# Small TensorE pieces in program order between blocks of matrix products: an attention, two-layer and expert kernel on one Trainium2 core

## The chip, the core and the metric

One NeuronCore of a Trainium2 chip runs the whole program; the other seven are idle. The metric is the device time of one execution in microseconds (us). TensorE multiplies, ScalarE (ACT in the profile), VectorE (DVE) and GpSimd (POOL) do the elementwise work, SyncE (SP) issues most DMAs.

## What is computed

All tensors are float32. Cut to what matters:

```python
def sm_attn(qq, kk, vv):
    s = scale * np.matmul(qq, kk.transpose(0, 1, 3, 2))
    a = softmax(s)
    return np.matmul(a, vv)
p_packed = sm_attn(p, k, v)              # 8 batches, 8 heads, 32 packed rows
x = sm_attn(q, p_packed, p_packed)       # 576 queries a batch -> 4608 tokens of 512
h = x @ w_in                             # 512 -> 2048
x = np.maximum(0.01 * h, h) @ w_out      # 2048 -> 512
logits = x @ w_gate                      # 8 experts
# greedy assignment, 576 tokens an expert, by falling logit
out[mask] = np.maximum(x[mask] @ w1[e], 0.0) @ w2[e]
```

## The kernel before

The program has four parts. `packs` makes the packed rows of all batches and folds them into `w_in` (tensor `wp` in DRAM). `tokens` (line 1383), which the change is about, does the query attention and the two layers for batches 0 to 5 and the first layer of batches 6 and 7. Then comes routing, in whose gaps TensorE does the second layer of batches 6 and 7 (`PutOff`), and last the eight experts.

Products are made exact enough by splitting each operand into a high and a low part and adding three products. In `tokens` the loops are batch `b` and, inside, 16 slices `f` of 128 of the 2048 hidden columns. For each slice:

- `mm1` (line 887): the first layer, 12 products of 288 columns (lines 54 to 56) into two PSUM banks of tile `h`; ScalarE copies them out, VectorE applies the slope, `split` (line 901) makes the halves `g`. This is a **block** of first-layer products.
- `mm2_list`: the second layer of the slice before, 12 products of 512 columns on even batches and 15 on odd ones (line 1044), into the accumulators `acc`, the fifth of which is the pool `a5` (tile `acc5`). Even batches do not use that fifth bank. They are queued in `todo`, and `emit` issues some.

Between the blocks lie **small pieces**, all of which pass through one PSUM bank, tile `x`:

- the query side of a later batch, `q_side` (line 783): per half, five pieces: two groups of four transposes of `rows` (line 547), two transposes of the tail (line 553), two score products (line 812, two each); then a softmax on ScalarE, VectorE and GpSimd (lines 820 to 836) into tile `at`, which that batch's `mm1` reads. GpSimd reorders the raw rows first (line 65).
- `times_gate` (line 1018): `turn` transposes 128 rows (line 1027), ScalarE copies them to `rowt` (line 1029), `product` multiplies by the gate weights (line 1034), VectorE copies the result to `L` or `wog` (line 1035). It is done for the finished rows of a batch (queue `dots`) and for 16 slices of `w_out` (queue `gates`, `wog_pieces`).
- `logits` (line 931): gate products for the batches whose second layer is put off; VectorE adds them to `lg` (line 956).

`evac` (line 993) copies the accumulators to `row` tiles at a batch's end. `side_unit` does `mm1` for batches 6 and 7 in the later slices of batches 4 and 5, and `SIDE_Q` says where their query sides are queued.

What sets the order: the program is recorded, and a list scheduler with a cost model orders each engine's instructions. In `tokens` it does so for TensorE too: `ordered(tc, MT)` with `MT` False leaves it free. Pieces are taken from the queues `qs`, `tabs`, `gates` and `dots` in the loop over `f`, one of each at a time.

Of the kernel before, what the change touches and what calls it, by code (L numbers as in the profile page):

```python
# [28 lines left out]
class Lag:  # L29
# [12 lines left out]

    def drain(self):
        self.pop(len(self.q))


def mm3(nc, ps, pairs, first=True, last=True):
# [431 lines left out]


LATE = 2
GPOP = 1
WI, WO, QS = 2, 5, 3
WOP = 2
W0 = 4
# [8 lines left out]
U6, U7 = 66, 84  # L494
LF = 16
DP = 0
SIDE_Q = [(2, 8), (4, 4)]


def SIDE(b, f):  # L500
# [253 lines left out]
class Tokens:  # L754
# [28 lines left out]
    def q_side(self, b, pool=None):  # L783

        nc, P = self.nc, self.P
        V, A, G, PE = nc.vector, nc.scalar, nc.gpsimd, nc.tensor
        st = {}

        def x_tile(shape):
            return P.ps.tile(shape, F32, name="x")  # L790

        def load(g):
            st[g] = load_rows(self.tc, nc, P.one, self.q, b, g, "")

        def rows(g):
            m, t = st[g]
            r = P.one.tile([128, 4, 4, 64], F32, name="rows")
            by_row(nc, r, m)
            qt = P.one.tile([128, 2, S], F32, name="kt", tag="kt")
            st["qt"] = qt  # L800
            st["fns"] = pairs_t(nc, qt, r, t, self.ident, x_tile, 64)
            st["fns"][0]()

        def sc(g, hf):
            qt = st["qt"]
            if hf == 0:
                t = P.two.tile([128, S], F32, name="soft", tag="soft")
                st["s"] = t
            ps = x_tile([128, HS])
            cs = slice(hf * HS, (hf + 1) * HS)  # L810
            for j in range(2):
                PE.matmul(ps[64 * j:64 * j + 64], self.cpp[:, b // 2, 2 * g + j, (b % 2) * 64:(b % 2) * 64 + 64],
                          qt[:, j, cs], start=True, stop=True)
            V.transpose(st["s"][:, cs], ps)

        def sm(g):
            nb = S // 32
            sf = st["s"]
            s = sf.rearrange("p (a b) -> p a b", b=32)
            mx = P.two.tile([128, nb], F32, name="mx2")  # L820
            V.reduce_max(mx, s, axis=AX.X)
            (G if PS & 1 else V).tensor_sub(s, s, mx.unsqueeze(2).to_broadcast([128, nb, 32]))
            A.activation(s, s, AF.Exp, scale=0.125)
            sm_ = P.two.tile([128, nb], F32, name="sm2")
            V.reduce_sum(sm_, s, axis=AX.X)
            V.tensor_scalar(sm_, sm_, 1e-9, None, op0=OP.add)
            V.reciprocal(sm_, sm_)
            (G if PS & 2 else V).tensor_mul(s, s, sm_.unsqueeze(2).to_broadcast([128, nb, 32]))
            e = P.two.tile([128, S], F32, name="soft", tag="soft")
            V.transpose(e, sf)  # L830
            if g == 0:
                t = (pool or P.two).tile([128, 2, 2, S], F32R, name="at2", tag="at2")
                st["at"] = t
            at = st["at"]
            A.copy(at[:, 0, g], e)
            V.tensor_sub(at[:, 1, g], e, f32(at[:, 0, g]))  # L836

        fns = [lambda: load(0)]
        for g in range(2):
            fns += [lambda g=g: rows(g), lambda: st["fns"][1](), lambda g=g: (st["fns"][2](), g == 0 and load(1)),  # L840
                    lambda g=g: sc(g, 0), lambda g=g: sc(g, 1), lambda g=g: sm(g)]
        return st, fns

    def open(self, keep, st):

        tc, nc = self.tc, self.nc

        def pool(st, name, bufs):
            return st.enter_context(tc.tile_pool(name=name, bufs=bufs, side="right"))

        self.wk5, self.wk3 = pool(keep, "t5", T1), pool(keep, "t3", 3)
        k1 = pool(keep, "k1", 1)
        self.lg, self.dots = {}, Lag()
# [77 lines left out]
    def logits(self, b, f, tf):  # L931
# [11 lines left out]
            nc.gpsimd.memset(t, 0.0)  # L943
            self.lg[b] = t
        lg = self.lg[b]
        ps = self.P.ps.tile([128, 192], F32, name="x")
# [67 lines left out]
    def gate(self, x, col):  # L1014

        self.dots.add(self.times_gate(lambda: x, lambda: self.L[:, col]))

    def times_gate(self, rows, out):

        nc, PE = self.nc, self.nc.tensor  # L1020
        st = {}

        def turn():
            x = rows()
            ps = self.P.ps.tile([128, 4, 128], F32, name="x")
            for c in range(4):
                PE.transpose(ps[:, c], x[:, c * 128:(c + 1) * 128], self.ident)
            st["t"] = self.two.tile([128, 4, 128], F32, name="rowt")
            nc.scalar.copy(st["t"], ps)

        def product():
            ps = self.P.ps.tile([128, E], F32, name="x")
# [3 lines left out]
        return [turn, product]  # L1036


def mm2_list(nc, acc, g, tl, wh, wl, start, stop):
# [343 lines left out]
def tokens(tk, pk, keep, first, st, acc_pools):  # L1383
# [5 lines left out]
    at = tk.first  # L1389
    tk.open(keep, st)  # L1390
    w = tk.w
    qs, tabs, gates = Lag(), Lag(), Lag()
    gates.add(tk.wog_pieces())
    tabs.add(tk.table_pieces)
    todo = []
    side = [(b, f) for b in range(B - ND, B) for f in range(NF)]
    sd = dict(at=[], w=None, next=0)

    def emit(n):
        for _ in range(min(n, len(todo))):  # L1400
            todo.pop(0)()

    def side_q():
        b = B - ND + len(sd["at"])
        at, fns = tk.q_side(b, tk.one)
        sd["at"].append(at)
        qs.add(fns)
        if b == B - ND:
            sd["w"] = tk.wp_load1(b, 0)

    def side_unit():
        b, f = side[sd["next"]]
# [9 lines left out]
    for b in range(B - ND):  # L1422
        if b == 1:
            first.close()
            tk.open_gate(keep, st)
        if b + 1 < B - ND:
            nat, fns = tk.q_side(b + 1)
            qs.add(fns)
        for f in range(NF):
            if b == 0 and f < NF - WOP:  # L1430
                for i in range(2):
                    tk.wout_piece(pk.w64, WOP + f, i)
            if f % 2 == 0:
                wcur = w
                nb, nf = (b, f // 2 + 1) if f // 2 < 7 else (b + 1, 0)
                if nb < B - ND:
                    if nb == 0:
                        pk.need(nf)
                    else:
                        pk.rest()  # L1440
                    w = tk.wp_load(nb, nf)
            t = tk.mm1(at, wcur, slice((f % 2) * 128, (f % 2) * 128 + 128))
            g, tl = tk.split(b, f, t)
            if b == 0:
                for _ in range(PI):
                    pk.piece()
                for _ in range(PP):
                    emit(PM)
                    pk.part()
            n = -(-len(qs.q) // (NF - f)) if b else QP  # L1450
            qs.pop(min(n, 1))
            if b:
                tabs.pop(1)
                gates.pop(GPOP)
            emit(len(todo) // 2)
            tk.dots.pop(1)
            if n > 1:
                emit(len(todo) // 2)
                qs.pop(n - 1)
            emit(len(todo))  # L1460
            if (b, f) == (B - ND - 1, LF):
                later.load(2)
            if f == 0:
                acc = sums(acc_pools, b)
            todo += mm2_list(nc, acc, g, tl, tk.wo(f, 0), tk.wo(f, 1), f == 0, f == NF - 1)
            if b == B - ND - 1:
                todo.append(lambda b=b, f=f, t=t: tk.logits(b, f, t))
            if f == NF - 1:
                todo.append(lambda b=b, acc=acc: tk.evac(b, acc, b < B - ND - 1))
            if (b, f) in SIDE_Q:  # L1470
                side_q()
            if SIDE(b, f):
                lg = side_unit()
                emit(len(todo) // 2)
                todo.append(lg)
        if b + 1 < B - ND:
            qs.drain()
            at = nat
    while sd["next"] < len(side):
        lg = side_unit()  # L1480
        emit(len(todo))
        tk.dots.pop(1)
        for _ in range(FTAIL):
            later.one()
        todo.append(lg)
    emit(len(todo))
    tk.dots.drain()
    return later


# [77 lines left out]
```

## Time and profile before

| | us |
|---|---|
| median of 3 runs (1464.46 to 1470.62) | 1464.66 |
| the profiled execution, its own time | 1474.13 |
| its span, first to last instruction | 1472.4 |
| TensorE busy in the span | 1381.9 |
| ScalarE, VectorE, GpSimd busy | 560.1, 742.3, 299.7 |
| mean granted TensorE clock, share of 2.4 GHz | 0.959 |

The page gives busy time by engine and the span in 40 slices. The windows view gives the same for chosen stretches; batches 1 to 5 of `tokens` lie between 258 and 864 us, routing between about 890 and 1020, the experts behind it. A busy TensorE is not TensorE at its peak: at the half clock the same product takes longer and still counts as busy.

### The profile page before, as it was taken

What the parts mean: (1) busy time and instruction counts of PE and PEld (TensorE: products, weight loads), DVE (VectorE), ACT (ScalarE), POOL (GpSimd) and SP (SyncE); (2) the same over time, 40 slices, a digit from 0 to 9 for tenths busy, and PEclk for the clock granted to TensorE, in tenths of its full rate; (3) what the DMA queues carried; (4) which work ended last, traced back from release to release, by engine and by line L of the source; (5) the groups of instructions that cost most, each with busy time, mean ns of one, the idle gap of its engine ahead of it and who ended that gap; (6) DMA issues with size and microseconds to landing.
All of it is one profiled execution on the core that took longest, in us unless ns stands there. A gap on an engine that the chain in (4) does not pass through costs nothing. (4 is left out here: it accounts for less than half of the span.)

```text
span 1472.4 us, 25686 instructions
## 1 busy us (share of the span) xinstructions
PE 1381.9 (94%) x10206; PEld 1150.2 (78%) x10206; DVE 742.3 (50%) x1878; ACT 560.1 (38%) x1209; POOL 299.7 (20%) x293
## 2 busy tenths in 40 slices
PE   7998898999998998899999988898999999999997
PEld 4666776887887886787788876676898989898986
DVE  4775798443343442356645566685444343433341
ACT  5665455433444443354544440101333332333331
POOL 3222224211212221232211120001221220220111
PEclk9999999998897997799999999998999999999999
DMA  9997655202102111133322354544643443443320
GB/s 272 292 276 222 196 170 179 81 29 66 35 30 71 43 37 49 45 122 121 129 76 93 109 196 160 158 141 124 198 124 106 129 136 108 136 116 100 122 72 36
DMA packets 147881, 180.49 MB, mean 123 GB/s; under 512 B 27952, under 2 KB 105776, under 8 KB 147760
## 3 DMA queue, kind: packets, MB, share of 16 engines
q1 hardware_dynamic: 122992, 141.08, 31.2%
q10 hardware_dynamic: 19008, 18.88, 4.3%
q0 software_dynamic: 5760, 18.88, 3.8%
q8 instruction: 81, 1.33, 0.4%
q14 instruction: 40, 0.33, 0.1%
HBM read 124.27 MB, written 54.53 MB: 121 GB/s over the span
## 5 line engine op out<-in xcount | busy, mean ns | idle before, releaser
L1044 PE MATMUL acc<-wout,g 128*128 128x512 f32 x1728 | 451.2, 406 | 14.8 <-ACT wout L778 5.5
L1044 PEld LDWEIGHTS acc<-wout,g 128*128 128x128 f32 x1728 | 316.5, 191 | 86.7 <-ACT wout L778 8.1
L898 DVE SCALAR_TENSOR_TENSOR t<-t 128x576 f32<-128x576 f32 x128 | 102.9, 804 | 142.8 <-ACT t L897 142.6
L897 ACT COPY t<-h 128x288 f32<-128x288 f32 x256 | 99.1, 400 | 169.2 <-PE h L56 147.7
L54 PE MATMUL h<-xt,w1hl 128*128 128x288 f32 x504 | 148.4, 294 | 1.4 <-DVE eg__12322 L1178 1.4
L55 PE MATMUL h<-xt,w1hl 128*128 128x288 f32 x504 | 148.5, 295 | 0.0
L56 PE MATMUL h<-xt,w1hl 128*128 128x288 f32 x504 | 148.4, 294 | 0.0
L54 PE MATMUL h<-at,wphl 128*128 128x288 f32 x384 | 122.2, 320 | 1.6 <-ACT t L897 1.4
L55 PE MATMUL h<-at,wphl 128*128 128x288 f32 x384 | 117.6, 306 | 0.2 <-DVE at L836 0.2
L56 PE MATMUL h<-at,wphl 128*128 128x288 f32 x384 | 116.3, 304 | 0.3 <-POOL wphl L875 0.3
L875 POOL TENSOR_TENSOR wphl<-wpraw,wphl 128x512 fp32r<-128x512 f32 x48 | 67.8, 1412 | 225.5 <-ACT wphl L874 225.3
L912 DVE TENSOR_TENSOR g<-t,g 128x512 fp32r<-128x512 f32 (+1 forms) x96 | 82.0, 854 | 42.7 <-ACT g L909 42.4
L54 PEld LDWEIGHTS h<-xt,w1hl 128*128 128x128 f32 x504 | 94.6, 188 | 4.3 <-ACT w1hl L1059 1.8
L55 PEld LDWEIGHTS h<-xt,w1hl 128*128 128x128 f32 x504 | 94.6, 188 | 2.4
L56 PEld LDWEIGHTS h<-xt,w1hl 128*128 128x128 f32 x504 | 94.5, 188 | 0.0
L1120 POOL DMA_INDIRECT xg<-x2d,idx x36 | 34.5, 960 | 289.7 <-PE x L1143 145.9
L54 PEld LDWEIGHTS h<-at,wphl 128*128 128x128 f32 x384 | 74.7, 196 | 9.5 <-ACT t L897 2.0
L909 ACT CAST g<-t 128x512 fp32r<-128x512 f32 (+1 forms) x96 | 64.7, 674 | 43.3 <-DVE t L898 42.4
L55 PEld LDWEIGHTS h<-at,wphl 128*128 128x128 f32 x384 | 75.2, 196 | 5.8 <-DVE at L836 0.9
L1183 POOL DMA_INDIRECT out_dram<-ot,idx x32 | 43.9, 1371 | 171.5 <-DVE ot L1196 163.9
L56 PEld LDWEIGHTS h<-at,wphl 128*128 128x128 f32 x384 | 74.9, 195 | 0.7 <-POOL wphl L875 0.5
L1070 DVE TENSOR_TENSOR w2hl<-w2raw,w2hl 128x1024 fp32r<-128x1024 f32 x31 | 37.9, 1224 | 59.6 <-ACT w2hl L1069 59.4
(778 smaller groups left out, 2444.9 us busy)
## 6 DMA issues: line engine op xcount, KB each, us to landing
gd<-g SPq DMA_DIRECT2D x32, 576.0 KB, 3.2
wp<-ev ACTq DMA_DIRECT2D x64, 256.0 KB, 4.8
w1raw<-in_moe_w_dram SPq DMA_DIRECT2D x30, 512.0 KB, 3.4
w2raw<-in_moe_w_dram SPq DMA_DIRECT2D x30, 512.0 KB, 3.6
wpraw<-wp SPq DMA_DIRECT2D x48, 256.0 KB, 2.9
g<-gd SPq DMA_DIRECT2D x16, 576.0 KB, 4.3
rawk<-in_k_dram SPq DMA_DIRECT2D x16, 512.0 KB, 5.8
rawv<-in_v_dram SPq DMA_DIRECT2D x16, 512.0 KB, 7.4
```

Source lines behind the costliest of these rows:

```text
L54: nc.tensor.matmul(ps, lh, rh, start=first and i == 0, stop=False)
L55: nc.tensor.matmul(ps, lh, rl, start=False, stop=False)
L56: nc.tensor.matmul(ps, ll, rh, start=False, stop=last and i == n - 1)
L875: nc.gpsimd.tensor_sub(w[:, 1], t, f32(w[:, 0]))
L897: A.copy(t[:, 64 + hf * HS:64 + (hf + 1) * HS], ps)
L898: V.scalar_tensor_tensor(t[:, 64:], t[:, 64:], 0.01, t[:, 64:], op0=OP.mult, op1=OP.max)
L909: A.copy(g[:, 0, c0:], tf[:, c0:])
L912: V.tensor_sub(g[:, 1, c0:], tf[:, c0:], f32(g[:, 0, c0:]))
L1044: mms.append(lambda: nc.tensor.matmul(acc[i], lhs, rhs, **kw))
L1070: sub(w[:, 1], t, f32(w[:, 0]))
L1120: self.nc.gpsimd.indirect_dma_start(out=t, out_offset=None, in_=self.x2d[:], in_offset=self.off(qb))
L1183: st = self.nc.gpsimd.indirect_dma_start(out=self.out, out_offset=self.off(qb), in_=t, in_offset=None)
```

## The change

From batch 1 on, `ordered(tk.tc, b > 0)` makes TensorE's instructions stand in the order in which the program records them; batch 0, the tail loop and all other engines stay with the scheduler. The loop body then says the order. `Pieces` is a queue whose entries may be marked as TensorE work by `pe`: `lead` runs the unmarked entries at its head, `take` gives one marked entry with the unmarked ones that follow it. For each slice a list `xs` is made: what must be done (`must`: logits), then pieces of the query side, so many that they are through by slice `QE` = 14, then `dots` and `gates` until the list has `XS` = 3. `small` issues one before `mm1`, one behind it, one in the middle of the second-layer products, and the rest at the end. The reorder of raw rows on GpSimd becomes an entry of its own (`turn`) ahead of the piece that reads it. The query sides of batches 6 and 7 are queued in batches 2, 3 and 4. In even batches, from slice 2 on, the gate pieces and logits take their bank from the accumulator pool `a5` (`bank`, `spare`); the query side stays with `x`. Tile `at2` of the side batches gets two buffers. Every product, copy and DMA is made as often as before.

```diff
+class Pieces(Lag):
+    def lead(self):
+        while self.q and not hasattr(self.q[0], "pe"):
+            self.q.pop(0)()
+    def take(self):
+        fns = []
+        while self.q and not (fns and hasattr(self.q[0], "pe") and any(hasattr(x, "pe") for x in fns)):
+            fns.append(self.q.pop(0))
+        return (lambda: [fn() for fn in fns]) if fns else None
...
-GPOP = 1
+QE, XS = 14, 3
...
-SIDE_Q = [(2, 8), (4, 4)]
+SIDE_Q = [[None], [None], [None, (6, 0)], [(6, 1), None], [None, (7, 0), (7, 1)], [None]]
...
-            fns += [lambda g=g: rows(g), lambda: st["fns"][1](), lambda g=g: (st["fns"][2](), g == 0 and load(1)),
-                    lambda g=g: sc(g, 0), lambda g=g: sc(g, 1), lambda g=g: sm(g)]
+            fns += [lambda g=g: turn(g), pe(lambda g=g: rows(g)), pe(lambda: st["fns"][1]()),
+                    pe(lambda g=g: (st["fns"][2](), g == 0 and load(1))),
+                    pe(lambda g=g: sc(g, 0)), pe(lambda g=g: sc(g, 1)), lambda g=g: sm(g)]
...
+    def bank(self, shape):
+        if self.spare:
+            return self.P.a5.tile(shape, F32, name="acc5")
+        return self.P.ps.tile(shape, F32, name="x")
...
-        for f in range(NF):
...
-            t = tk.mm1(at, wcur, slice((f % 2) * 128, (f % 2) * 128 + 128))
-            g, tl = tk.split(b, f, t)
...
-            n = -(-len(qs.q) // (NF - f)) if b else QP
-            qs.pop(min(n, 1))
-            if b:
-                tabs.pop(1)
-                gates.pop(GPOP)
-            emit(len(todo) // 2)
-            tk.dots.pop(1)
-            if n > 1:
-                emit(len(todo) // 2)
-                qs.pop(n - 1)
...
+        with ordered(tk.tc, b > 0):
+            for f in range(NF):
...
+                tk.spare = b > 0 and b % 2 == 0 and 2 <= f
+                xs = must[:]
+                must.clear()
+                if b:
+                    tabs.pop(1)
+                    for x in (qs, tk.dots, gates):
+                        x.lead()
+                    left = sum(hasattr(x, "pe") for x in qs.q)
+                    xs += [x for x in (qs.take() for _ in range(-(-left // max(1, QE - f)))) if x]
+                    for more in (tk.dots, gates):
+                        while len(xs) < XS:
+                            x = more.take()
+                            if x is None:
+                                break
+                            xs.append(x)
...
+                small()
+                t = tk.mm1(at, wcur, slice((f % 2) * 128, (f % 2) * 128 + 128))
+                g, tl = tk.split(b, f, t)
...
+                small()
+                emit(len(todo) // 2)
+                small()
+                if SIDE(b, f):
+                    must.append(side_unit())
+                    small()
+                emit(len(todo))
...
+                small(len(xs) - 1)
...
+                small(len(xs))
```

How the order moves, at two places. Names: `h` and `acc` are PSUM tiles of the first and second layer, `x` the small pieces' bank, a number behind a name one buffer. Lines of the change's own numbering: 572 and 578 are the query transposes (547 and 553 before), 841 the scores (812), 1065 and 1072 `turn` and `product` (1027 and 1034), 1082 the second layer (1044).

TensorE at the end of batch 3 and the start of batch 4, before; left out are six first-layer products:

```order
L1044 MATMUL acc_5163<-wout_1962,g 128x512
L812 MATMUL x<-kt,cpp 64x288 x2
L1034 MATMUL x<-wg,rowt 128x8 x4
L812 MATMUL x<-kt,cpp 64x288 x2
L1027 MATMUL x<-ident,wsum 128x128 x4
L1027 MATMUL x<-ident,row 128x128 x4
L1034 MATMUL x<-wg,rowt 128x8 x8
...
L547 MATMUL x<-ident,rows 128x128 x4
L1027 MATMUL x<-ident,row 128x128 x4
L547 MATMUL x<-ident,rows 128x128 x4
L1027 MATMUL x<-ident,wsum 128x128 x4
L1034 MATMUL x<-wg,rowt 128x8 x4
```

The same place with the change; left out are the first layer's blocks of 12:

```order
L1082 MATMUL acc_5216<-wout_1962,g 128x512
...
L572 MATMUL x<-ident,rows 128x128 x4
L1082 MATMUL acc<-wout_1962,g 128x512 x8
...
L578 MATMUL x<-ident,rawtail 128x64 x2
...
L841 MATMUL x<-kt,cpp 64x288 x2
L1082 MATMUL acc<-wout_88,g 128x512 x6
L1065 MATMUL x<-ident,row 128x128 x4
L1082 MATMUL acc<-wout_88,g 128x512 x6
```

Before, some twenty small pieces stand one behind the other with half a block of the first layer among them; with the change each has a block of the first or half a block of the second layer on either side.

TensorE inside batch 2, before, between two first-layer blocks:

```order
L1044 MATMUL acc<-wout_88,g 128x512 x11
L1034 MATMUL x<-wg,rowt 128x8 x4
L1044 MATMUL acc<-wout_88,g 128x512
...
L1044 MATMUL acc<-wout_88,g 128x512 x7
L1034 MATMUL x<-wg,rowt 128x8 x4
```

The same batch with the change; `acc_4571` and `acc_4584` are tiles in the lent bank:

```order
L1065 MATMUL acc_4571<-ident,row 128x128 x4
L1082 MATMUL acc<-wout_88,g 128x512 x6
L1072 MATMUL acc_4584<-wg,rowt 128x8 x4
L1082 MATMUL acc<-wout_88,g 128x512 x6
L572 MATMUL x<-ident,rows 128x128 x4
```

Before, a slice holds about one small piece; now it holds up to three, and the transposes of a row block and the product that needs their copy are six second-layer products apart.

## Rows read from the trace of the kernel before

**Rows 1.** Page, parts 1 and 2: busy time, TensorE's granted clock in 40 slices.

```profile
PE 1381.9 (94%) x10206; PEld 1150.2 (78%) x10206; DVE 742.3 (50%) x1878; ACT 560.1 (38%) x1209; POOL 299.7 (20%) x293
...
PEclk9999999998897997799999999998999999999999
```

**Rows 2.** Windows of batches 1 to 5 and routing; first line names the columns.

```profile
core 0: us, PE busy (x) PEld busy (x) DVE busy (x) ACT busy (x) POOL busy (x), PEclk, DMA share, GB/s
258.30:358.40 100.10, 100.10 (x566) 86.12 (x564) 38.35 (x54) 43.45 (x100) 21.45 (x18) 1.00 0.17 51
358.40:381.00 22.60, 18.33 (x76) 14.76 (x76) 9.04 (x16) 7.95 (x18) 5.07 (x5) 0.55 0.18 61
459.60:480.00 20.40, 15.99 (x66) 11.57 (x66) 8.76 (x24) 7.42 (x18) 3.59 (x3) 0.58 0.25 83
569.50:609.70 40.20, 30.16 (x125) 23.02 (x125) 12.08 (x26) 10.63 (x22) 7.99 (x7) 0.53 0.16 51
609.70:731.00 121.30, 118.90 (x804) 100.08 (x806) 71.52 (x132) 64.27 (x155) 32.41 (x30) 1.00 0.32 107
731.00:863.50 132.50, 130.99 (x999) 109.89 (x997) 69.72 (x148) 60.74 (x139) 22.77 (x23) 1.00 0.29 102
863.50:1020.00 156.50, 141.33 (x2296) 107.80 (x2295) 109.07 (x447) 18.02 (x41) 7.72 (x12) 0.96 0.53 164
```

**Rows 3.** The same view, TensorE's products of tile x alone: the small pieces.

```profile
258.30:358.40 100.10, 13.61 (x102) 1.00 0.17 51
358.40:381.00 22.60, 13.35 (x56) 0.55 0.18 61
459.60:480.00 20.40, 11.14 (x48) 0.58 0.25 83
569.50:609.70 40.20, 26.98 (x110) 0.53 0.16 51
```

**Rows 4.** The same view, tile h alone: first layer's products in batch 1.

```profile
258.30:358.40 100.10, 31.28 (x199) 1.00 0.17 51
```

**Rows 5.** Timeline of TensorE in batch 1: start us, us, instruction, count.

```profile
343.67 3.43 PE L1044 MATMUL acc<-wout,g 128*128 128x512 f32 x14
...
346.93 0.29 PE L54 MATMUL h<-at,wphl 128*128 128x288 f32 x1
...
347.32 0.29 PE L54 MATMUL h<-at,wphl 128*128 128x288 f32 x1
```

**Rows 6.** Timeline of TensorE, batches 3 to 4; idle us and releaser in brackets.

```profile
588.59 1.09 PE L1027 MATMUL x<-ident,wsum 128*128 128x128 f32 x4 [0.77 <-ACT kt L548]
590.41 1.88 PE L1034 MATMUL x<-wg,rowt 128*128 128x8 f32 x8 [0.73 <-ACT rowt L1029]
592.55 0.47 PE L553 MATMUL x<-ident,rawtail 64*128 64x64 f32 x2 [0.26 <-DVE L L1035]
593.37 1.88 PE L1034 MATMUL x<-wg,rowt 128*128 128x8 f32 x8 [0.35 <-ACT kt L554]
```

**Rows 7.** Waits of TensorE from 609.7 to 863.5 us: total us, times, longest.

```profile
PE h L54 <- ACT t L897: 2.0, 4, 0.6
```

**Rows 8.** Lines, 258.3 to 358.4 us: count | busy us, mean ns | idle.

```profile
L1029 ACT COPY rowt<-x 128x512 f32<-128x512 f32 x6 | 3.5, 587 | 2.5 <-PE x L1027 2.5
...
L814 DVE STREAM_TRANSPOSE soft<-x 128x288 f32<-128x288 f32 x2 | 1.0, 484 | 3.3 <-PE x L812 3.3
...
L828 POOL TENSOR_TENSOR soft<-soft,sm 128x576 f32<-128x576 f32 x1 | 1.2, 1162 | 2.8 <-PE h L56 2.8
...
L830 DVE STREAM_TRANSPOSE soft<-soft 128x576 f32<-128x576 f32 x1 | 0.8, 778 | 1.3 <-POOL soft L828 1.3
...
L825 DVE TENSOR_REDUCE sm<-soft 128x18 f32<-128x576 f32 x1 | 0.8, 753 | 0.0
...
L823 ACT ACTIVATE soft<-soft 128x576 f32<-128x576 f32 x1 | 0.7, 685 | 1.0 <-DVE soft L822 1.0
...
L1035 DVE COPY L<-x 128x8 f32<-128x8 f32 x3 | 0.5, 162 | 3.4 <-PE x L1034 3.4
```

More of the change, by code (lines that the diff above doesn't have):

```diff
@@ L44, in drain, with pe, piece @@
         self.pop(len(self.q))
+class Pieces(Lag):
[7 more added lines that the diff above has]
+        return (lambda: [fn() for fn in fns]) if fns else None
+def pe(fn):
+    def piece():
+        return fn()
+    piece.pe = True
+    return piece
 def mm3(nc, ps, pairs, first=True, last=True):
@@ L793, in load, with turn @@
             st[g] = load_rows(self.tc, nc, P.one, self.q, b, g, "")
-        def rows(g):
+        def turn(g):
             m, t = st[g]
@@ L798, in rows @@
             by_row(nc, r, m)
+            st["r"] = r
+        def rows(g):
+            r, t = st["r"], st[g][1]
             qt = P.one.tile([128, 2, S], F32, name="kt", tag="kt")
@@ L831, in sm @@
             if g == 0:
-                t = (pool or P.two).tile([128, 2, 2, S], F32R, name="at2", tag="at2")
+                t = (pool or P.two).tile([128, 2, 2, S], F32R, name="at2", tag="at2", bufs=2)
                 st["at"] = t
@@ L852, in open @@
         k1 = pool(keep, "k1", 1)
-        self.lg, self.dots = {}, Lag()
+        self.lg, self.dots = {}, Pieces()
         self.wout.append(k1.tile([128, self.NF // 2, 2, D], F32R, name="wout1"))
@@ L945, in logits @@
         lg = self.lg[b]
-        ps = self.P.ps.tile([128, 192], F32, name="x")
+        ps = self.bank([128, 192])
         w = self.wog[:, f]
@@ L1016, in gate @@
         self.dots.add(self.times_gate(lambda: x, lambda: self.L[:, col]))
+    def bank(self, shape):
+        if self.spare:
+            return self.P.a5.tile(shape, F32, name="acc5")
+        return self.P.ps.tile(shape, F32, name="x")
+    spare = False
     def times_gate(self, rows, out):
@@ L1024, in turn @@
             x = rows()
-            ps = self.P.ps.tile([128, 4, 128], F32, name="x")
+            ps = self.bank([128, 4, 128])
             for c in range(4):
@@ L1031, in product @@
         def product():
-            ps = self.P.ps.tile([128, E], F32, name="x")
+            ps = self.bank([128, E])
             for c in range(4):
@@ L1035, in product @@
             nc.vector.tensor_copy(out(), ps)
-        return [turn, product]
+        return [pe(turn), pe(product)]
 def mm2_list(nc, acc, g, tl, wh, wl, start, stop):
@@ L1391, in tokens @@
     w = tk.w
-    qs, tabs, gates = Lag(), Lag(), Lag()
+    qs, tabs, gates = Pieces(), Lag(), Pieces()
     gates.add(tk.wog_pieces())
@@ L1395, in tokens @@
     todo = []
+    must = []
     side = [(b, f) for b in range(B - ND, B) for f in range(NF)]
     sd = dict(at=[], w=None, next=0)
+    put = {}
     def emit(n):
@@ L1401, in emit, with side_q @@
             todo.pop(0)()
[L1403 to L1409, printed above, removed]
+    def side_q(b, g):
+        if g == 0:
+            at, fns = tk.q_side(b, tk.one)
+            sd["at"].append(at)
+            put[b] = fns
+            if b == B - ND:
+                sd["w"] = tk.wp_load1(b, 0)
+        n = len(put[b]) // 2 + 1
+        qs.add(put[b][:n] if g == 0 else put[b][n:])
     def side_unit():
@@ L1425, in tokens @@
             tk.open_gate(keep, st)
-        if b + 1 < B - ND:
-            nat, fns = tk.q_side(b + 1)
-            qs.add(fns)
-        for f in range(NF):
[L1430 to L1441, printed above, removed]
-            t = tk.mm1(at, wcur, slice((f % 2) * 128, (f % 2) * 128 + 128))
-            g, tl = tk.split(b, f, t)
[L1444 to L1449, printed above, removed]
-            n = -(-len(qs.q) // (NF - f)) if b else QP
-            qs.pop(min(n, 1))
-            if b:
-                tabs.pop(1)
-                gates.pop(GPOP)
-            emit(len(todo) // 2)
-            tk.dots.pop(1)
-            if n > 1:
-                emit(len(todo) // 2)
-                qs.pop(n - 1)
-            emit(len(todo))
[L1461 to L1473, printed above, removed]
-                emit(len(todo) // 2)
-                todo.append(lg)
@@ L1476, in tokens, with small @@
[L1476 to L1480, printed above, removed]
-        emit(len(todo))
[L1482 to L1487, printed above, removed]
+        for q in SIDE_Q[b]:
+            if q:
+                side_q(*q)
+            elif b + 1 < B - ND:
+                nat, fns = tk.q_side(b + 1)
+                qs.add(fns)
+        with ordered(tk.tc, b > 0):
+            for f in range(NF):
+                if b == 0 and f < NF - WOP:
+                    for i in range(2):
+                        tk.wout_piece(pk.w64, WOP + f, i)
+                if f % 2 == 0:
+                    wcur = w
+                    nb, nf = (b, f // 2 + 1) if f // 2 < 7 else (b + 1, 0)
+                    if nb < B - ND:
+                        if nb == 0:
+                            pk.need(nf)
+                        else:
+                            pk.rest()
+                        w = tk.wp_load(nb, nf)
+                tk.spare = b > 0 and b % 2 == 0 and 2 <= f
[13 more added lines that the diff above has]
+                            xs.append(x)
+                def small(n=1):
+                    for _ in range(min(n, len(xs))):
+                        xs.pop(0)()
+                small()
+                t = tk.mm1(at, wcur, slice((f % 2) * 128, (f % 2) * 128 + 128))
+                g, tl = tk.split(b, f, t)
+                if b == 0:
+                    for _ in range(PI):
+                        pk.piece()
+                    for _ in range(PP):
+                        emit(PM)
+                        pk.part()
+                    qs.pop(min(len(qs.q), QP))
+                small()
+                emit(len(todo) // 2)
+                small()
[3 more added lines that the diff above has]
+                emit(len(todo))
+                if (b, f) == (B - ND - 1, LF):
+                    later.load(2)
+                small(len(xs) - 1)
+                if f == 0:
+                    acc = sums(acc_pools, b)
+                todo += mm2_list(nc, acc, g, tl, tk.wo(f, 0), tk.wo(f, 1), f == 0, f == NF - 1)
+                if b == B - ND - 1:
+                    must.append(lambda b=b, f=f, t=t: tk.logits(b, f, t))
+                if f == NF - 1:
+                    todo.append(lambda b=b, acc=acc: tk.evac(b, acc, b < B - ND - 1))
+                small(len(xs))
+            tk.spare = False
+            if b + 1 < B - ND:
+                qs.drain()
+                at = nat
@@ new lines, in tokens @@
+    with ExitStack():
+        while sd["next"] < len(side):
+            xs = must[:]
+            must.clear()
+            lg = side_unit()
+            for x in xs[:1]:
+                x()
+            emit(len(todo))
+            for x in xs[1:]:
+                x()
+            for i in range(FTAIL):
+                if i == FTAIL // 2:
+                    tk.dots.pop(1)
+                later.one()
+            must.append(lg)
+        emit(len(todo))
+        for x in must:
+            x()
+        tk.dots.drain()
```

## The prediction

> **What bounds the kernel now.** Read the page first. TensorE is busy 1381.9 of 1472.4 us and no other engine comes near [rows 1], so time is saved only by making TensorE idle less or run faster. The clock line of the same page shows where: in most slices the granted clock is 9 tenths or more, and from the 10th to the 17th it sags to 7 and 8 [rows 1]. The windows view, cut at those places, tells the rest [rows 2]. Batch 1 (258.3 to 358.4 us) runs with TensorE busy throughout and a granted clock of 1.00, the 2.4 GHz level. Then come three stretches of 22.6, 20.4 and 40.2 us with clocks of 0.55, 0.58 and 0.53, that is, nearly all at the 1.2 GHz level, in which TensorE is also idle for 4.3, 4.4 and 10.0 us. They lie at the ends of batches 1, 2 and 3. From 609.7 us on the clock is 1.00 again, with 2.4 and 1.5 us idle in two windows of 121.3 and 132.5 us.
>
> What does TensorE do in the three stretches? Of its 76, 66 and 125 products there, 56, 48 and 110 belong to tile `x` [rows 2, 3]: the small pieces that were left over when the batch's blocks were gone. The timeline shows why they crawl [rows 6]: each waits 0.26 to 0.77 us for ScalarE or VectorE to empty the one bank, then runs at the slow level, 1.8 to 2.1 us from one start to the next. In batch 1, where blocks lie between them, the same pieces cost little and make nothing idle.
>
> So the question is not what the pieces cost, but where they stand. By the order, the change puts each of them between blocks and leaves none at a batch's end.
>
> **The sum.** First the price of a small piece among blocks, from batch 1. A second-layer product starts 0.233 us after the one before it (14 from 343.67 to 346.93), a first-layer product 0.13 us after (three from 346.93 to 347.32) [rows 5]. Batch 1's window has 566 products [rows 2], of which 199 are first layer [rows 4] and 102 small [rows 3]; the other 265 are second layer. 265 x 0.233 = 61.7 us and 199 x 0.13 = 25.9 us leave 12.5 us of the 100.1 for 102 small products: 0.122 us each, handovers included.
>
> With that price the contents of the three stretches, spread among blocks, would cost:
> - first: 56 x 0.122 + 20 x 0.13 = 9.4 us of 22.6; 13.2 us freed.
> - second: 48 x 0.122 + 18 x 0.13 = 8.2 of 20.4; 12.2 us freed.
> - third: 110 x 0.122 + 15 x 0.13 = 15.4 of 40.2; 24.8 us freed [rows 2, 3].
>
> Together **50.2 us freed**. Nothing is computed less; the whole gain is waits covered by blocks and work moved from the slow level to the fast one.
>
> Against it stand **new waits**. In strict order TensorE cannot pass a piece whose input or bank is late. The cover is good: between two pieces stand a first-layer block (12 x 0.13 = 1.6 us) or six to eight second-layer products (1.4 to 1.9 us). A bank is free again after ScalarE's copy (0.59 us), VectorE's transpose (0.48) or its small copy (0.16) [rows 8], if that engine comes at once. It will not always: on ScalarE a cast of `g` may stand ahead, on VectorE a softmax. The nearest rows are those of batches 4 and 5, where logits and pieces already share one bank among blocks: TensorE idles 3.9 of 253.8 us, 1.5% [rows 2], half of it before a first-layer block [rows 7]. Batches 1 to 5 take 605.2 us now and about 555 after; 1.5% of that is 8.5 us, of which 3.9 are there already, so I take 4.6 us. The ends of the bound: nothing, as in batch 1, or 0.5 us at every piece, as at the batch ends (a rival, below).
>
> Edits that I cost at nothing: the queues' bookkeeping is done while recording; GpSimd's reorder of rows, now its own entry, stands before its piece and its input is loaded a half ahead in SyncE's order; the lent bank in even batches and the second `at2` buffer take waits away and add none, since the odd batch's accumulator needs the bank only a slice later; the earlier query sides of batches 6 and 7 are the same work, among the same blocks. The query side of the next batch now ends around slice 11, so its softmax (GpSimd's product alone is 1.16 us [rows 8]) is hidden by the last slices instead of holding the next batch's first block. Batch 0 and the packs before it stay with the scheduler, but it orders a few pieces otherwise there; I take zero, and 5 us either way for the range. Routing and experts start earlier and are otherwise the same; routing, with TensorE busy 141.3 of 156.5 us [rows 2], follows directly on the last logits.
>
> Sum: 50.2 - 4.6 = 45.6 us. The profiled execution took 1474.13 us, so 1428.5. The median of the runs, 1464.66, is 0.9936 of the profiled time; in the same proportion the forecast is **1419 us**.
>
> **A rule against the change.** The rows show the clock falling where TensorE ran only small pieces with a wait before each, and staying at 1.00 where pieces lay among blocks [rows 2, 6]. The Trainium skill, in TensorE: Matmul & The Clock Gate, section "A second HAM failure mode: psum-queue depth-cycling", tells of the opposite danger: small idles between groups of products, while PSUM banks are cycled, make the clock swing between its two levels all through a kernel. By that rule the change, which hands a bank over in every slice, could slow the dense batches too; by the rows, which have such handovers in batch 1 at a clock of 1.00, it does not. The sum goes by the rows.
>
> **Rivals.**
> - *Softmax chains hold the bank* (1443 us). VectorE empties the bank in its own fixed order. If that copy stands behind a softmax step that waits for GpSimd, it is late by the chain of exponent, sum, product and transpose: 0.69 + 0.75 + 1.16 + 0.78 = 3.4 us [rows 8], of which six second-layer products cover 1.4. Six query sides have two halves each: 12 x 2.0 = 24 us given back, 1452.5 profiled. For it: TensorE can no longer step aside. Against it: the scheduler still orders VectorE by when things are ready.
> - *A convoy: slower* (1507 us). There are some 176 small pieces from batch 1 to 5: ten for each of six query sides, two for each of 16 slices of `w_out` and 22 row tiles, some 40 logits. If each waits as at the batch ends, 0.53 us in the mean of four rows [rows 6], 93 us are paid for 50.2 gained: 1517 profiled. It decides from 0.29 us a piece. Against it: at the batch ends no block lay between; here at least 1.4 us does, against a release of 0.6.
> - *Nothing comes through* (1465 us). The tokens end sooner, but the next stage waits as long as the gain, for a load or a chain of VectorE. Against it: routing needs only the logits, and its put-off products read what was stored long before.
> - *More than the sum* (1405 us). No new wait, the 3.9 us of batches 4 and 5 go too, and so do a few us of idle in batch 0 and before routing (clock 0.96 there [rows 2]): about 60 us.
> - That the change does not do what it says is ruled out by the order: the pieces do stand between blocks.
>
> **Chances.** Forecast 0.56, softmax chains 0.19, more than the sum 0.12, convoy 0.07, nothing 0.06. A measurement of this kernel can tell about 0.5% (7 us) from no change. So faster 0.87, same 0.06, slower 0.07. The range from 1402 to 1446 us holds the first three with 3 us at either end, since batch 0's 5 us would seldom add to an extreme.
>
> **What would show it.** In the changed profile: (1) a clock of 1.00 from about 258 us to the end of batch 5 and no stretch of small pieces alone; if a clock near 0.5 stands at a batch's end, the first step is wrong. (2) Batches 1 to 5 in about 560 us instead of 605. (3) Waits of TensorE on ScalarE and VectorE below 10 us there in all; if before `x` pieces they total 25 us or more, with VectorE's `soft` or GpSimd behind them, the first rival holds; if every piece has one, the convoy. (4) Routing and experts as long as before, within a few us; if they are longer by what the tokens lost, the gain was only moved.

## The result, and the profile after

| | before | after |
|---|---|---|
| median of the runs, us | 1467.64 (1464.46 to 1471.74, 4 runs) | 1415.05 (1410.42 to 1417.32, 4 runs) |
| profiled execution, us | 1474.13 | 1415.55 |
| ratio to before | | 0.9636, 95% interval 0.9597 to 0.9676 |

Faster by 3.6%, 52.6 us between the medians. The forecast was 1419 us.

The page of the changed kernel, parts 1 and 2, beside [rows 1]:

```profile
PE 1347.5 (95%) x10206; PEld 1126.1 (80%) x10206; DVE 732.4 (52%) x1878; ACT 559.5 (40%) x1209; POOL 309.1 (22%) x293
...
PEclk9999999999999999999999999997999999999999
```

The same 10206 products keep TensorE busy for 34.4 us less, and the sag of the clock from the 10th to the 17th slice is gone. The one lower slice lies between routing and experts, where the kernel before has one too.

The windows view of the changed kernel: batches 1 to 5 one by one, each from its first product on, then routing, then the experts.

```profile
core 0: us, PE busy (x) PEld busy (x) DVE busy (x) ACT busy (x) POOL busy (x), PEclk, DMA share, GB/s
250.10:362.20 112.10, 112.10 (x695) 97.19 (x693) 40.75 (x70) 46.87 (x106) 42.29 (x31) 1.00 0.14 42
362.20:450.20 88.00, 88.00 (x515) 73.52 (x514) 41.91 (x75) 42.65 (x100) 18.08 (x14) 1.00 0.18 58
450.20:545.20 95.00, 95.00 (x532) 78.72 (x531) 42.59 (x64) 42.00 (x94) 17.99 (x14) 1.00 0.16 53
545.20:675.50 130.30, 127.30 (x870) 105.80 (x868) 80.89 (x142) 71.90 (x169) 36.06 (x32) 1.00 0.34 116
675.50:803.20 127.70, 125.69 (x947) 105.58 (x946) 63.13 (x137) 55.93 (x129) 22.81 (x22) 1.00 0.28 100
803.20:957.00 153.80, 139.77 (x2296) 106.12 (x2295) 109.65 (x449) 19.38 (x44) 8.39 (x13) 0.98 0.51 164
957.00:1413.80 456.80, 437.82 (x2619) 392.42 (x2616) 170.50 (x319) 134.51 (x193) 82.31 (x72) 0.97 0.36 116
```

Batch 1's first products mix with batch 0's last second-layer products, and not in the same way in every kernel, so batches 1 to 5 as a whole are cut elsewhere: from the first copy of batch 0's accumulators (its `evac`) to the first copy of batch 5's. By that cut, the change:

```profile
255.30:803.20 547.90, 542.89 (x3518) 456.03 (x3518) 266.40 (x483) 256.92 (x589) 133.16 (x107) 1.00 0.23 77
```

and the kernel before, followed by its routing and its experts:

```profile
266.00:861.60 595.60, 572.90 (x3512) 480.68 (x3511) 269.35 (x483) 257.40 (x587) 125.54 (x106) 0.94 0.21 71
861.60:1018.00 156.40, 141.23 (x2302) 107.24 (x2301) 110.40 (x451) 19.25 (x44) 8.72 (x13) 0.96 0.52 162
1018.00:1472.40 454.40, 436.25 (x2621) 390.54 (x2619) 170.38 (x319) 134.87 (x194) 82.30 (x72) 0.98 0.38 117
```

Batches 1 to 5 took 595.6 us and take 547.9, which is 47.7 less. (The prediction's 605.2 us have other ends, 258.3 and 863.5.) TensorE's idle time there falls from 22.7 us (595.6 - 572.9) to 5.0, and its busy time by 30.0 us at a clock of 1.00 in all five batches in place of a mean of 0.94. Batch 1 has more products than before (695), since it now takes most of the `w_out` pieces, and nothing is left at any batch's end. Routing and experts together take 610.6 us against 610.8. The rest of the difference between the two profiles, 10.7 us, was won ahead of that cut: the first copy of batch 0 starts at 255.3 us in place of 266.0. That was not forecast.

A slice of batch 1 in the changed kernel's timeline (TensorE; rows of the first layer left out):

```profile
299.93 0.60 PE L1065 MATMUL x<-ident,wsum 128*128 128x128 f32 x4
300.29 1.87 PE L1082 MATMUL acc<-wout,g 128*128 128x512 f32 x7
302.00 0.95 PE L1072 MATMUL x<-wg,rowt 128*128 128x8 f32 x8
302.80 2.11 PE L1082 MATMUL acc<-wout,g 128*128 128x512 f32 x8
304.84 0.71 PE L841 MATMUL x<-kt,cpp 128*64 128x288 f32 x4
305.48 0.40 PE L78 MATMUL h<-at,wphl 128*128 128x288 f32 x1
```

No row has a wait in brackets. The four transposes delay the next product by 0.36 us (299.93 to 300.29), the eight products with gate weights by 0.80.

The price of a small product can be worked out as in the prediction, from the products of each tile in batch 1's window:

```profile
250.10:362.20 112.10, 35.23 (x264) 1.00 0.14 42
```

These 264 are the small ones; 193 are first layer and 238 second layer. 112.1 - 238 x 0.233 - 193 x 0.13 leaves 31.6 us, 0.12 us each, as in the kernel before.

### The profile page after: what moved, and what is told of

Its sections match the earlier page's. It is cut to its first block, busy times and chain, and to the rows that moved or that the text cites. A ratio compares the mean times of both kernels' runs of the same rounds, so it can differ in the third digit from the quotient of the medians.

```text
span 1413.8 us, 25670 instructions
## 1 busy us (share of the span) xinstructions
PE 1347.5 (95%) x10206; PEld 1126.1 (80%) x10206; DVE 732.4 (52%) x1878; ACT 559.5 (40%) x1209; POOL 309.1 (22%) x293
## 5 line engine op out<-in xcount | busy, mean ns | idle before, releaser
L78 PE MATMUL h<-at,wphl 128*128 128x288 f32 x384 | 123.7, 322 | 0.6 <-ACT t L927 0.6
L79 PE MATMUL h<-at,wphl 128*128 128x288 f32 x384 | 114.0, 297 | 0.0
L80 PE MATMUL h<-at,wphl 128*128 128x288 f32 x384 | 113.7, 297 | 0.0
L78 PEld LDWEIGHTS h<-at,wphl 128*128 128x128 f32 x384 | 73.0, 190 | 14.1 <-issue 7.9
L79 PEld LDWEIGHTS h<-at,wphl 128*128 128x128 f32 x384 | 73.1, 190 | 0.8
L80 PEld LDWEIGHTS h<-at,wphl 128*128 128x128 f32 x384 | 72.7, 190 | 0.1
```

What stands on the lines that cost most here:

```text
L78: nc.tensor.matmul(ps, lh, rh, start=first and i == 0, stop=False)
L79: nc.tensor.matmul(ps, lh, rl, start=False, stop=False)
L80: nc.tensor.matmul(ps, ll, rh, start=False, stop=last and i == n - 1)
```

## The experiments

Each kernel but the first was timed against the kernel before on the same chip.

| kernel | median, us | ratio to before (95% interval) |
|---|---|---|
| before_again | 1469.41 (one run) | |
| no_lent | 1414.84 | 0.9623 (0.9583 to 0.9662) |
| free_order | 1451.36 | 0.9879 (0.9838 to 0.9919) |
| strict_before | 1486.40 | 1.0104 (1.0064 to 1.0143) |
| bunched | 1505.51 | 1.0232 (1.0172 to 1.0292) |
| q_last | 1428.07 | 0.9705 (0.9673 to 0.9736) |
| old_b0 | 1428.20 | 0.9708 (0.9673 to 0.9744) |
| old_pop | 1415.48 | 0.9627 (0.9593 to 0.9660) |
| merge_q0 | 1427.21 | 0.9699 (0.9670 to 0.9727) |
| merge_q1 | 1417.40 | 0.9639 (0.9614 to 0.9664) |
| q0_values_acc | 1420.37 | 0.9671 (0.9649 to 0.9692) |
| preload | 1413.47 | 0.9623 (0.9601 to 0.9645) |

### before_again: is the picture of before stable?

> The kernel before, once more, for a second profile: it tells how far batch 0 and the packs move from run to run. If the 10 us by which batch 0 ended earlier with the change are run-to-run noise, the last first-layer block of batch 0's successor starts anywhere from 250 to 258 us here; if they come from the change, it starts at 258 us again. Both readings expect stretches at about half clock at the ends of batches 1, 2 and 3, some 70 us in sum, and 1462 to 1474 us.

Windows of this second profile: batches 1 to 5, cut at the copies, then the three stretches at their ends.

```profile
263.00:858.80 595.80, 573.12 (x3512) 480.82 (x3511) 269.07 (x483) 257.67 (x587) 125.61 (x106) 0.94 0.22 71
357.80:378.30 20.50, 17.41 (x69) 14.51 (x70) 8.53 (x15) 7.05 (x15) 5.38 (x5) 0.50 0.08 22
460.20:477.20 17.00, 14.43 (x56) 10.54 (x56) 8.62 (x23) 5.54 (x14) 2.34 (x2) 0.50 0.13 36
569.40:607.00 37.60, 28.42 (x113) 21.94 (x114) 11.57 (x24) 9.73 (x19) 8.02 (x7) 0.50 0.12 38
```

The batches take 595.8 us, as before, with the three stretches at half clock in the same places. What lies ahead of them moves by about 3 us from run to run: batch 1's first product starts at 255.5 us in place of 258.3, which the expectation had counted as noise. But the first evac starts at 263.0 us here, at 266.0 in the first profile and at 255.3 with the change, so this run alone leaves open how much is noise; `old_b0` below settles it.

### no_lent: is it the second bank?

```diff
-                tk.spare = b > 0 and b % 2 == 0 and 2 <= f
+                tk.spare = False
```

> Of the change, only the lent PSUM bank is taken away: all small pieces use the one bank x. If the block between two pieces (1.4 us or more) hides the handover (0.6 us), nothing is lost: 1413 to 1420 us, clock 1.00 through batches 2 and 4. If the second bank is what carries the gain, batches 2 and 4 show waits at each gate piece, 0.3 us or more at each of 40 pieces: 1428 us or more.

1414.8 us. Batch 2, in which gate pieces and query pieces now share one bank (windows view):

```profile
360.40:448.50 88.10, 88.10 (x517) 73.55 (x516) 41.93 (x75) 42.62 (x100) 18.10 (x14) 1.00 0.18 58
```

TensorE is never idle in it, and the batch takes 88.1 us against 88.0. With a block between two pieces, one bank is enough, and the lent bank contributes nothing that can be measured.

### free_order: is writing the pieces out evenly enough?

```diff
-        with ordered(tk.tc, b > 0):
+        with ordered(tk.tc, False):
```

> The loop body of the change, but TensorE's order left to the scheduler again. If it is the strict order that keeps pieces among blocks, the scheduler moves them again and stretches of pieces alone come back at batch ends: 1440 to 1468 us, with a granted clock near 0.5 there. If writing the pieces out evenly is enough, the time stays at 1413 to 1420 us.

1451.4 us. Windows at the end of batch 1, and of batches 1 to 5, cut at the copies:

```profile
340.30:367.10 26.80, 21.18 (x99) 16.95 (x98) 6.63 (x14) 7.98 (x16) 7.11 (x6) 0.68 0.16 54
252.20:829.50 577.30, 558.40 (x3510) 471.30 (x3508) 271.91 (x481) 256.15 (x588) 126.53 (x106) 0.96 0.22 73
```

The scheduler again leaves pieces over: 26.8 us with 99 products at a clock of 0.68. Batches 1 to 5 take 577.3 us, 18.3 less than before and 29.4 more than with the change. So the even recording by itself brings over a third of the gain in the batches, and the strict order the rest. The whole kernel is about 18 us faster than before in its median: 11 to 14 us are won ahead of the first copy here too (252.2 us, against 263.0 and 266.0; below), and in this profile routing and experts take 5 us longer (616.0 us behind 829.5, against 610.8).

### strict_before: is strictness enough?

```diff
+        strict = ExitStack()
+        strict.enter_context(ordered(tk.tc, b > 0))
         for f in range(NF):
...
+        strict.close()
```

(in the kernel before; its loop body is unchanged)

> The loop body of before, but TensorE in program order from batch 1 on. Its recording takes one entry of each queue a slice, so strictness alone should already leave few pieces over at a batch's end: 1418 to 1435 us by my theory, a little above the change for pieces that stand next to each other and wait for the bank. If the new spacing (one piece between blocks, query side first) is what matters, the waits and the slow stretches stay: 1450 us or more.

My expectation failed: 1486.4 us, slower than before. Windows of batches 1 to 5, cut at the copies, then the longest waits of TensorE there:

```profile
265.10:871.40 606.30, 557.86 (x3513) 467.12 (x3512) 270.82 (x482) 258.53 (x589) 137.05 (x107) 0.98 0.21 69
```

```profile
PE x L949 <- DVE lg L956: 17.4, 12, 1.8
PE x L1027 <- DVE soft L814: 5.7, 6, 1.1
PE x L1034 <- ACT kt L548: 4.8, 5, 1.3
PE x L1027 <- ACT kt L548: 3.8, 4, 1.2
```

Strictness did spread the pieces: the mean clock rises from 0.94 to 0.98 and TensorE's busy time falls by 15.0 us. But idle time rises from 22.7 to 48.4 us. A slice of batch 1 shows where (TensorE's timeline, rows in a row):

```profile
289.26 0.71 PE L812 MATMUL x<-kt,cpp 128*64 128x288 f32 x4
291.00 0.66 PE L1027 MATMUL x<-ident,wsum 128*128 128x128 f32 x4 [1.04 <-DVE soft L814]
291.41 1.86 PE L1044 MATMUL acc<-wout,g 128*128 128x512 f32 x7
293.12 0.95 PE L1034 MATMUL x<-wg,rowt 128*128 128x8 f32 x8
```

In the old loop body a gate piece follows a query piece with nothing between and waits 1.04 us for the bank; the row piece has seven second-layer products before it and waits for nothing. In batches 4 and 5 one to three products lie between such pieces, and logits often follow logits directly (12 waits, 17.4 us). The scheduler used to order these pieces by its own cost model; now TensorE waits for the bank wherever too little stands between two of them.

### bunched: spread over slices, but side by side

```diff
-                small()
+                small(len(xs))
                 t = tk.mm1(at, wcur, slice((f % 2) * 128, (f % 2) * 128 + 128))
```

> The change, but all pieces of a slice stand next to each other ahead of its first-layer block; they are spread over the slices as in the change. If a block between two pieces is what hides the handover of the bank, the second and third piece of a slice each wait about 0.5 us: some 96 of them, 48 us, 1450 to 1470 us, and the granted clock stays at 1.00 for nearly all of batches 1 to 5. If spreading over the slices is enough (no stretch of pieces alone), 1413 to 1425 us.

1505.5 us, 90 more than the change by one line, and above both expected ranges. Windows of batch 1 and of batches 2 to 5, then a slice of batch 1 in TensorE's timeline:

```profile
250.00:410.00 160.00, 140.16 (x691) 118.76 (x691) 40.46 (x70) 49.70 (x105) 35.50 (x30) 0.84 0.10 30
410.00:902.50 492.50, 450.46 (x2853) 376.11 (x2851) 231.96 (x417) 214.92 (x488) 91.80 (x80) 0.97 0.23 77
```

```profile
297.36 0.60 PE L572 MATMUL x<-ident,rows 128*128 128x128 f32 x4
298.63 0.66 PE L1065 MATMUL x<-ident,wsum 128*128 128x128 f32 x4 [0.68 <-ACT kt L573]
299.96 1.06 PE L1072 MATMUL x<-wg,rowt 128*128 128x8 f32 x8 [0.68 <-ACT rowt L1067]
300.88 0.52 PE L78 MATMUL h<-at,wphl 128*128 128x288 f32 x1
301.20 0.44 PE L79 MATMUL h<-at,wphl 128*128 128x288 f32 x1
301.44 0.44 PE L80 MATMUL h<-at,wphl 128*128 128x288 f32 x1
```

The waits came as expected: TensorE is idle 61.9 us in batches 1 to 5 (652.5 - 590.6), 0.68 us before the second and the third piece of the slice shown. What I had not expected is the clock. It does not stay at 1.00: in batch 1 its mean is 0.84, and the rows show it falling behind the bunch, where first-layer products start 0.24 us apart in place of 0.13. Busy time is 42.5 us more than with the change (590.6 against 548.1).

Whether the waits or the row of small products by itself brings the clock down, these runs do not separate.

Together, `bunched`, `strict_before` and the change show both halves of the mechanism: to spread pieces over the slices is not enough, a block between two of them is.

### q_last: does the query side have to come first?

```diff
-                    xs += [x for x in (qs.take() for _ in range(-(-left // max(1, QE - f)))) if x]
-                    for more in (tk.dots, gates):
+                    for more in (tk.dots, gates, qs):
```

> The change, but the three places of a slice go to the finished rows and the w_out gate pieces first and to the query side last. In batch 1 those fill all places, so the query side of batch 2 is left over: some nine pieces alone at its end, about 1.8 us each, and a softmax that batch 2's first block waits for: 15 to 30 us more, 1430 to 1445 us, with one stretch at half clock there. If the order of the queues does not matter, 1412 to 1420 us.

1428.1 us, 13 more than the change, just under the range that I expected. Windows of the boundary of batches 1 and 2, then the longest wait of TensorE for another engine there:

```profile
366.10:376.30 10.20, 5.04 (x17) 4.42 (x18) 3.64 (x8) 3.40 (x7) 2.35 (x2) 0.50 0.00 0
```

```profile
PE h L78 <- ACT at L864: 5.3, 1, 5.3
```

One boundary loses what was expected of it: the first block of batch 2 waits 5.3 us for the last step of the late softmax, at a clock of 0.50.

### old_b0, old_pop, merge_q0, merge_q1: the time won ahead of batch 1

`old_b0` writes the packs and batch 0 as before:

```diff
+            head = [lambda g=g: (turn(g), rows(g))] if b < 2 else [lambda g=g: turn(g), pe(lambda g=g: rows(g))]
...
-                    qs.pop(min(len(qs.q), QP))
+                    qs.pop(1)
                 small()
                 emit(len(todo) // 2)
+                if b == 0:
+                    emit(len(todo) // 2)
+                    qs.pop(QP - 1)
                 small()
```

`old_pop` has the second part of this diff alone; `merge_q0` and `merge_q1` the first part alone, with `b == 0` and `b == 1` for `b < 2`.

The expectations, in the order of the heading:

> The change, but with the packs and batch 0 written as before: GpSimd's row reorder together with its first transposes for the query sides of batches 0 and 1, and the pieces taken one, then two a slice; TensorE's order is then that of before up to the end of batch 0. The profiles so far put the end of batch 0 (its first evac) at 252 to 255 us with the change's batch 0 and at 263 to 266 us without. If that comes from the reorder, this kernel takes 1423 to 1427 us and its first evac is at 262 us or later; if it is drift between runs, 1412 to 1418 us.

> Half of that: the row reorder stays an entry of its own, but batch 0 takes its pieces one, then two a slice as before. If the entry of its own (which lets the scheduler start GpSimd and the raw loads otherwise) makes the 9 to 10 us, 1412 to 1418 us; if the taking of three at once makes them, 1422 to 1427 us.

> The change, but the row reorder stands together with its first transposes again in the query side of batch 0 alone, which is issued during the packs. The 12 us that the split gives fall 3 us before batch 0 and 8 to 9 in it. If they come from the packs, where a query piece in bank x stands ahead of the packs' own products (loads of v wait on those products 16 us against 6), this kernel takes 1422 to 1430 us. If they come from batch 0's own order, 1412 to 1418 us.

> The same with the query side of batch 1 alone, which is issued in batch 0. If the packs make the 12 us, 1412 to 1418 us; if batch 0's own order, 1422 to 1430 us.

`old_b0` 1428.2, `old_pop` 1415.5, `merge_q0` 1427.2, `merge_q1` 1417.4 us. The windows view of `old_b0` has batches 1 to 5, cut at the copies, in this row:

```profile
265.90:813.80 547.90, 542.87 (x3518) 455.73 (x3517) 266.71 (x485) 256.96 (x589) 133.61 (x109) 1.00 0.24 77
```

They take 547.9 us, exactly as with the change. What differs lies ahead of them: the first copy of batch 0 starts at 265.9 us here and at 266.6 in `merge_q0`, against 255.3 with the change, 254.4 in `old_pop` and 257.0 in `merge_q1`. So 10 to 13 us of the change's gain come from one detail: GpSimd's row reorder for batch 0's query side is an entry of its own, and since the packs issue two entries a round, every query piece of that side moves to another place among the packs' products. Batch 0's own order and the three at once give nothing that can be measured. The remaining change, `old_b0`, is 2.9% faster than before.

Why the place matters is partly seen. From 30 to 122 us SyncE waits for the packs' value products (tile `x`, the bank that query pieces use) before it can reload `v`. The waits view of SyncE and the windows view from 40 to 80 us, first of `merge_q0`, then of the change:

```profile
SPq L597 <- PE x L766: 13.7, 7, 6.1
```

```profile
40.00:80.00 40.00, 37.07 (x429) 23.99 (x426) 33.08 (x79) 25.54 (x68) 12.29 (x14) 1.00 0.97 278
```

```profile
SPq L597 <- PE x L766: 7.1, 8, 2.9
```

```profile
40.00:80.00 40.00, 38.79 (x414) 26.46 (x414) 29.56 (x78) 28.11 (x77) 13.91 (x16) 1.00 1.09 313
```

The loads wait 6.6 us less for these products with the change, and the DMA engines move 313 GB/s in place of 278 in this window.

### q0_values_acc: is it the shared bank?

```diff
-        ps = P.ps.tile([128, 64], F32, name="x")
+        ps = psum(P, [128, 64])
```

(in `merge_q0`)

> The kernel of merge_q0 (1427 us), with the packs' value products in a bank of the acc pool in place of x, so that a query piece in x cannot stand ahead of them. If that shared bank is how the merged reorder costs 12 us, the wait of SyncE's loads of v on those products shrinks from 14 to about 7 us between 30 and 122 us and the time goes to 1413 to 1419 us. If it is something else in the packs' order, 1424 us or more.

1420.4 us, between the two. The same two views:

```profile
SPq L597 <- PE acc L766: 7.6, 6, 2.5
```

```profile
40.00:80.00 40.00, 39.94 (x429) 24.91 (x425) 29.64 (x80) 26.29 (x69) 12.94 (x15) 1.00 0.98 283
```

The wait on these products shrank as expected, and 7 of 12 us came back, but the DMA rate stayed at 283 GB/s, and the same loads now wait 4.8 us for other products of the packs in the banks of `acc` (line 714). The bank may have a part in it; the scheduler also made another order of everything behind it, so how large a part stays open.

### preload: the next wait

```diff
-LF = 16
+LF = 15
...
-        self.wk5, self.wk3 = pool(keep, "t5", T1), pool(keep, "t3", 3)
+        self.wk5, self.wk3 = pool(keep, "t5", T1), pool(keep, "t3", 4)
```

> The change with the first two loads of the put-off second layer moved from its start to slice 15 of batch 5, and a fourth buffer of g for them. In all profiles TensorE waits about 5 us for these loads where routing begins, next to a short stretch at half clock. If that wait is on the path, 5 us less: 1408 to 1412 us; if routing's own chain on VectorE sets its end, no difference: 1413 to 1418 us.

1413.5 us (1412.8 to 1418.7), not to be told from the change. In its profile the wait for the put-off loads (5.1 us in the change's) does not appear, but the first copy of batch 0 starts 3.4 us later than with the change, so a gain of a few us in routing would not show in the total. Whether that wait sets routing's end stays open. No version was found that beats the change measurably.

## Why the prediction was right, and where it was short

- **The stretches at the batch ends: right.** They were priced at 50.2 us freed, 45.6 after new waits. Batches 1 to 5 became shorter by 47.7 us in the profile, 17.7 of it idle time and 30.0 busy time, and by the same 47.7 (595.6 - 547.9) with the packs and batch 0 as before (`old_b0`). The step is the one forecast and its size within about 2 us; the price of a small product, 0.122 us, came out at 0.12 in batch 1 after the change.
- **New waits: sized too large.** I took 4.6 us on top of the 3.9 of batches 4 and 5. In all, 5.0 us are idle now, 1.1 more. With 47.7 net that leaves 48.8 freed, so the 50.2 was too large by 1.4 and the waits by 3.5; the two errors partly cancel. The waits of TensorE in batches 1 to 5 of the changed kernel, longest first, beside [rows 7]:

```profile
PE acc L979 <- DVE t L928: 3.0, 3, 1.2
PE x L1065 <- DVE lg L986: 1.0, 1, 1.0
PE x L996 <- DVE lg L986: 1.0, 1, 1.0
```

- **Softmax chains: did not come.** None of the rows has a softmax tile; all are logits or pieces behind them, in batches 4 and 5. The premise that VectorE would hold a bank behind GpSimd for 2 us a half is not seen once.
- **The convoy: it came in another kernel.** The rival was put at 1507 us, a wait of 0.53 us at every piece. `bunched` is close to that kernel and takes 1505.5, but that the totals agree is luck: its waits are about 62 us in place of 93, the lower clock adds 42.5 us that the rival did not have, and the gain ahead of batch 1 is in it too. The premise that a block of at least 1.4 us stands between pieces is what kept the change from it.
- **The rule on the clock.** The rows of `bunched` show the clock falling to its lower level inside dense batches, behind pieces that waited 0.68 us each. With the change, five batches of bank handovers, nearly all without a wait, stay at 1.00. The Trainium skill, TensorE: Matmul & The Clock Gate, section "A second HAM failure mode: psum-queue depth-cycling", tells of a clock that swings where TensorE idles briefly between groups of products; the rows of `bunched` agree with it (0.84 in batch 1), and the change leaves too few such idles (5.0 us in all) to show it.
- **The lent bank: right** that it costs nothing, and it also brings nothing (`no_lent`).
- **The packs and batch 0: the step that was missed.** "I take zero, and 5 us either way." `old_b0` measures 13 us (1428.2 against 1415.1), 10.6 of which its profile shows ahead of batch 0's first copy. An entry more in a queue that is issued two at a time moved a whole chain of pieces among the packs. The order showed that TensorE's instructions differ from the 46th row on; I treated that as noise, and it was about a quarter of the gain. Without it the change is worth 2.9% against a forecast of 3.1% (45.6 of 1474.13 us): 1428 us, 9 above the forecast. Of these 9 us, 5.6 are the kernel before itself, which took 1470.2 us beside `old_b0` and 1464.66 in the runs that the forecast started from; the other 3.6 are a gain of 42.0 in place of 45.6 us, although the batches alone gave 47.7. So that 1415 lies so near to 1419 is in part luck: a term taken at zero made up for both.
- **The rest: right.** Routing and experts kept their 610.6 us; the rival in which a later stage eats the gain is out.

What stays open: how the place of the query pieces acts on the packs, and how much of that is the shared bank.

## What to carry to other kernels

Where small pieces share one bank, price them twice from the same trace: among blocks (here 0.12 us a product, 0.5 us for a piece of four) and alone (about 1.8 us a piece from one start to the next, most of it wait and half clock), and look for where the second price is paid: at the ends of loops, where the work that hid them is gone. Here a strict order paid only together with spacing: between any two pieces a block at least as long as the release of the bank (1.4 us or more against 0.6). Strictness alone made this kernel slower, and spacing alone brought over a third of the gain in the batches. And when a queue is issued by counts, splitting an entry moves everything behind it, so read that place of the order too.

## What was not expected of the hardware

Three pieces side by side in each slice, with waits of 0.3 to 1.5 us between them, were enough to pull TensorE's mean granted clock in batch 1 to 0.84. The same pieces, one by one between blocks, leave it at 1.00. And in the packs, the rate of the DMA engines went with the order of the pieces: 313 GB/s against 278 between 40 and 80 us, though the transfers of the whole kernel are the same. It is not the measure of the time, since `q0_values_acc` won back most of the difference at 283 GB/s.
